# A remade head and a spread decay in a kernel that joins linear attention with a gelu layer

## The chip, the cores and the metric

The kernel runs on one core of one Trainium2 chip. Its time is the device time of one execution in microseconds, and the median of several executions is compared. A profile of one execution shows each instruction on the five engines and the transfers. The engines are TensorE (PE, with PEld for its weight loads), VectorE (DVE), ScalarE (ACT), GpSimd (POOL) and SyncE (SP).

## The reference

```python
# q, k, v: (4, 8, 768, 64); lam: (8,); block = 64
for b in range(nb):
    intra = einsum('bhic,bhjc->bhij', qb, kb) * Dmask
    intra = einsum('bhij,bhjd->bhid', intra, vb)
    inter = einsum('bhid,bhde->bhie', qb * lam_pow, kv_state)
    out[:, :, sl] = intra + inter
    kv_state = lam_block * kv_state + einsum('bhsd,bhse->bhde', kb * rev_pow, vb)
# then, with x of (3072, 512), w_in (512, 2048) and w_out (2048, 512):
h = x @ w_in
return (0.5 * h * (1.0 + erf(h / sqrt(2)))) @ w_out
```

Linear attention with a decay for each head gives x. Two matrix products with a gelu between them follow. The state `kv_state` is the only thing that one block of the sequence hands to the next.

## The kernel before, in words

The sequence of 768 is cut into six groups of 128 positions. A group holds all four batches, so it has 512 tokens. Per group the kernel makes transposed copies of q and k, scores on TensorE, masked scores on DVE, outputs on TensorE, the scaled outputs `x_t` on DVE, then the first layer (`mm1`), the gelu on ACT, and the second layer (`mm2`). State products (k against scaled v, `vs`) give the next group's states; from group 1 on DVE adds them to the old states in `tmp`, and ACT multiplies them by the decay (`decay`, L306, four instructions, one for each pair of heads).

There is no scheduler at run time. Each engine works its own instructions in the order in which the program text emits them, and that order is written by hand in strings, one letter per action:

- `LOADS1` is the order on POOL in the head: `K Q V` load group 0 (the digit is the pair of batches), `k q v` group 1, `i` and `w` load parts of w_in and w_out, `m` makes a part of the mask `m_p` for the second half of the heads (L171), and `s` scales v (L199). Each load of q, k or v is two DMAs of 128 KB, and each of w_in or w_out is one of 256 KB. All go through the one software queue of POOL. The first k and q are issued ahead of the string.
- `HEAD` is the order of group 0: `K`, `Q` transposes (L316), `S` scores (L349), `O` outputs (L370) and `x_t`, `z` the first state products (L393), `m` and `n` blocks of eight first-layer matmuls (L725) for the first and second pair of batches, `M` masks of the first half, `d` decay tables, `g` a one-element gelu, and `.` an idle matmul (L711) whose result nobody reads. It stands where TensorE would otherwise wait.
- `PHASE1` runs group 0's second layer in 16 parts (`p`, four matmuls of 512 columns, L505) among group 1's attention (`k q s o`), sums of weights on DVE (`i`, `w`, `t`) and scalings of v on ACT (`h`).
- `PHASE2` runs group 1's first layer (`m`, `n`) among group 2's attention and the loads of group 3 (`K Q V`). `z` and `Z` are the state products of groups 1 and 2, `y` and `Y` the decays behind them, and `c` a transpose by DMA on SP's queue.
- `PA`, `PB`, `PC` are the periods of groups 2, 3 and 4, and 5. In each, `a` is a product of four matmuls (L526) of the group's own first layer and `m` one of four (L688) of the second layer of the group before, both in a form with seven products in place of eight. `v` is a visit of the next group's attention, `h` scales v, `x` makes sums on DVE. The digits of `L2S` and `LA` are lags, counted in slots, by which DVE's sums are put behind.

Within a period's unit, product 5 writes bank uV, which ACT copies to `Vs` (L556). Product 1 writes uY, which ACT copies into uV (L548, the seed). Product 6 writes uY again, and so waits for the seed.

Of the kernel before, what the change touches and what calls it, by code (L numbers as in the profile page):

```python
# [7 lines left out]
F32 = mybir.dt.float32  # L8
# [6 lines left out]
def kernel(  # L15
# [11 lines left out]
    B, H, S, D = q.shape  # L27
# [3 lines left out]
    HP = H // 2  # L31
# [16 lines left out]
    V, A, P, G, SY = nc.vector, nc.scalar, nc.tensor, nc.gpsimd, nc.sync  # L48

    def bank(tag, shape, dtype=F32, name=None):  # L50
        return ps.tile(shape, dtype, tag=tag, name=name or "p_" + tag, bufs=1)


    done = set()
# [22 lines left out]
    def flush():  # L77
        while later_list:
            x = min(later_list)
            later_list.remove(x)  # L80
            x[2]()


    raw = {}
    dram = dict(q=q, k=k, v=v)

    def load(g, pair, name):
        if pair == 0:
            raw[g, name] = raw_pool.tile([128, B, H, D], BF16, tag="r" + name, name="raw_" + name, bufs=1 if name == "q" else 2)
        t = raw[g, name].rearrange("p (n a) h d -> p n (a h d)", n=2)[:, pair].rearrange("p (h t d) -> p h t d", h=H, t=2)  # L90
        for b in range(2):
            G.dma_start(t[b * 64:(b + 1) * 64].rearrange("p h t d -> p h (t d)"),
                        dram[name][2 * pair + b, :, g * C:(g + 1) * C, :].rearrange("h (p t) d -> p h (t d)", t=2))
        raw[g, pair, name] = t
# [30 lines left out]
    idle = consts.tile([128, 256], BF16)  # L125
# [24 lines left out]
    for hi in range(2):  # L150
        p = slice(hi * D, (hi + 1) * D)
# [36 lines left out]
    def new_x(g):  # L188
        xs[g] = x_pool.tile([128, HP, B, C], BF16, tag="x", name="x_t")
# [111 lines left out]
                decay(g + 1, raw["tmp", g])  # L301
        later(lag, add)

    def decay(g, tmp):
        for hp in range(HP):
            A.activation(states[g][:, :, hp, :], tmp[:, :, hp, :], ACT.Copy, scale=lam_c[:, hp:hp + 1])  # L306
        done.add(("st", g))


    def p_transposes(g, pair, name, tag, engs):  # L310
# [100 lines left out]
    def new_g(g):  # L411
        gts[g] = g_pool.tile([128, NK2, T], BF16, tag="g", name="g_t")

    def new_gs(g):
        gs[g] = [None if i == 2 else g_pool.tile([128, NK2 // 2, T // 2], BF16, tag=f"gs{i}", name=f"gs{i}", bufs=2) for i in range(4)]
        gs[g][2] = gts[g][:, 0:NK2 // 2, T // 2:]
# [28 lines left out]
    def sums_x(g, i):  # L445

        x = xs[g]
        if i == 3:
            t_x[g] = [x_pool.tile([128, 2, T // 2], BF16, tag=f"tx{i}", name=f"tx{i}", bufs=2) for i in range(4)]
        t1, t2, t3, t4 = (t.rearrange("p k (s c) -> p k s c", s=2) for t in t_x[g])  # L450
        b11, b12, b21, b22 = x[:, 0:2, 0:2], x[:, 0:2, 2:4], x[:, 2:4, 0:2], x[:, 2:4, 2:4]
        need(("x", g, 2), ("x", g, 3))
        if i != 3:
            need(("x", g, 0), ("x", g, 1))
        if i == 3:
            V.tensor_sub(t3, b22, b12)
        elif i == 1:
            V.tensor_sub(t1, b12, b11)
        elif i == 2:
            need(("tx", g, 1))  # L460
            V.tensor_sub(t2, b22, t1)
        else:
            need(("tx", g, 2))
            V.tensor_sub(t4, b21, t2)
        done.add(("tx", g, i))
# [227 lines left out]
        return slots  # L693


    LOADS1 = "Q1 m1 i0 V0 K1 m0 V1 i4 i1 i5 s0 i2 i3 w0 s1 i7 i6 k0 q0 w1 w4 w2 w5 k1 q1 v0 v1 w6 w3 w7"
    HEAD = "b . . . . . . . . . . . . . . . . . . . . . . . . . . . . K M M . . . . . . . Q d . . . . . . . S . S Q . . . . . . . . . . . . . . . . . . . . . . . . O . . . . . . . . . K . . . . . S . . . . . . . S . . m g O z . m n n n n m m m n m m n n n m"

    def script(text, actions):
        for word in text.split():  # L700
            fn = actions[word]
            (fn.pop(0) if isinstance(fn, list) else fn)()

    tags = ["uY", "uV", "uZ"]
    idle_ps = {}

    def idle_bank(tag):
        idle_ps[0] = bank(tag, [128, 512], F32, "idle_ps")

    def keep_warm():  # L710
        P.matmul(idle_ps[0][:, 0:256], idle[:, :128], idle, start=True, stop=True)  # L711

    part_no = [0]

    def mm1_part(g, i, pair, lag=None):

        need(*[("x", g, 2 * pair + b) for b in range(2)])
        h = bank(tags[part_no[0] % 3], [128, 2, 256])
        part_no[0] += 1
        x = xs[g].rearrange("p k s c -> p k (s c)")  # L720
        w = slice(256 * pair, 256 * pair + 256)
        for j in range(2):
            kf = 2 * i + j
            for ki in range(NK1):
                P.matmul(h[:, j, :], w_in_t[:, ki, kf * 128:(kf + 1) * 128], x[:, ki, w],  # L725
                         start=(ki == 0 and j == 0), stop=True, skip_group_check=True)
        A.activation(gts[g][:, 2 * i:2 * i + 2, w], h, ACT.Gelu)
        done.add(("gp", g, i, pair))
        u = i % 4
        if lag and all(("gp", g, x, y) in done for x in (u, u + 4) for y in range(2)):  # L730
            done.update(("g", g, u, n) for n in "XYZW")
            for n, j in enumerate((1, 2, 4, 3)):
                later(int(lag[4 * u + n]), lambda j=j: sums_g(g, u, j))
        tick()

    new_x(0)
    new_g(0)
    for item in LOADS1.split():
        i = int(item[1:])
# [8 lines left out]
        else:  # L748
            load(int(item[0].islower()), i, item[0].lower())
    script(HEAD, {  # L750
        ".": keep_warm,
# [33 lines left out]
        "z": lambda: p_state_products(1, ("a0", "a1")),  # L785
        "y": lambda: decay(2, raw["tmp", 1]),
    }
    PHASE1 = "i i p w i k q i p p w p s k q p p p t s p p w t s h h o w p p p s p p o p p"
    script(PHASE1, attn_1)


# [11 lines left out]
    new_g(1)  # L803
    new_gs(1)
    new_x(2)
    L2S = "2792133901460230"
    PHASE2 = "q z m k y n s q m n h s k n K m s o m n t V n s t Q h m n c c o x c M Z m c x m n m x x n Y"

    def digits(text, i, n):
        return [int(c) for c in text[i * n:(i + 1) * n]]  # L810

    script(PHASE2, {
        "m": [lambda i=i: mm1_part(1, i, 0, L2S) for i in (0, 4, 1, 5, 2, 6, 3, 7)],
        "n": [lambda i=i: mm1_part(1, i, 1, L2S) for i in (0, 4, 1, 5, 2, 6, 3, 7)],
        "w": attn_1["w"],
# [11 lines left out]
        "y": attn_1["y"],  # L827
        "M": mask_n,
        "Z": lambda: p_state_products(2, ab),
        "Y": lambda: decay(3, raw["tmp", 2]),  # L830
        "x": [lambda i=i: sums_x(2, i) for i in (3, 1, 2, 4)],
    })
    flush()

    PA = "mQKamammahmaavamaahmhahhmhmhmamhmaavammcVaaccmavmammmmaavcaaamavmamamaxaxxmmamxm"
    PB = "hQaKahhhhvmhmhhmVamvmaamamamamammaammacvacamamamccmavamammamavamamxmaamaaxxmammx"
    PC = "KQahamhvhhhmhhmVhmamamammaaavmmamamaacamcvmaacmcammvamaaammaamvammaaxmmaamxmmxax"
    LA = "2201000002202032034341212002332000200000022"  # L840
    LB = "2010000142522221213032570306003201000104020"
    LC = "0000001010210242003020330213002101104202001"
    for g in range(2, NG):
        seqs, lag = {2: (PA, LA), 5: (PC, LC)}.get(g, (PB, LB))
        LZ, LW, LS, LM, LV = lag[0:4], lag[4:8], lag[8:24], lag[24:28], lag[28:43]
        new_g(g)
        m2 = mm2_slots(g - 1, dict(M=digits(LM, 0, 4)))
        new_gs(g)
        att = g + 1 < NG
        if att:  # L850
            new_x(g + 1)
        assert seqs.count("a") == seqs.count("m") == 28
        a = []
        for u in range(4):
            sl = dict(zip("5162734", unit_slots(g, u, dict(Z=int(LZ[u]), W=int(LW[u]), S=digits(LS, u, 4)))))
            a += [sl[c] for c in ("1562734" if u == 0 else "5162734")]
        cross = list(CROSS)
        visits = list(range(5))
        sums = [3, 1, 2, 4]
        heads = list(range(H))  # L860
        for c in seqs:
            if c == "a":
                a.pop(0)()
                tick()
            elif c == "m":
                m2.pop(0)()
                tick()
            elif c == "v":
                i = visits.pop(0)
                if att:  # L870
                    visit(g + 1, i, digits(LV, i, 3))
            elif c in "KQV":
                if g + 2 < NG:
                    load_group(g + 2, c.lower())
            elif c == "c":
                x = cross.pop(0)
                if g + 2 < NG:
                    crossbar(g + 2, *x)
            elif c == "h":
                h = heads.pop(0)  # L880
                if att:
                    scale_v_group(g + 1, h)
            elif c == "x":
                i = sums.pop(0)
                if att:
                    sums_x(g + 1, i)
        assert not (a or m2 or visits or sums or heads or cross)
        flush()
    for s in mm2_slots(NG - 1, dict(M=(0, 0, 0, 0))):
        s()  # L890
# [32 lines left out]
```

## Time and profile before

| What | Value |
| --- | --- |
| median of 3 runs | 209.7 us (209.05 to 211.25) |
| the profiled execution | 210.08 us |
| its span, first to last instruction | 208.3 us |
| granted clock of TensorE, mean | 0.998 |
| busy: PE, DVE, ACT, POOL | 96%, 68%, 58%, 29% |
| instructions in the profile | 6283 |

The profiled execution's time is 1.8 us longer than the span, for what lies ahead of the first and behind the last instruction. A row of a timeline gives start, length, engine, line, operation, tiles and the number of merged instructions, and in brackets the engine's idle time ahead of it with what ended it. A row of the chain gives start, length and what. "issue" there is time in which an engine waited for nothing that the profile shows. A DMA row gives issues, the size of each and the median time from issue to landing.

### The profile page before, as it was taken

To read this page: it belongs to the slowest core of one execution; us is meant where nothing else is said; L and a number is where in the kernel's file an instruction comes from. 1 tells how busy PE (TensorE), PEld (TensorE's weight loads), DVE (VectorE), ACT (ScalarE), POOL (GpSimd) and SP (SyncE) were. 2 spreads that over 40 slices of the span, in tenths; PEclk is the share of its full clock that TensorE was granted. 3 is DMA by queue.
4 is the path that set the end of the run, shared out by engine and by line. 5 is a ranking of instruction groups with operands and counts; after the bars stand their busy time and mean duration, and the time that the engine had idled before them with its cause. 6 is when DMAs were issued, how large, how long until landed. Compare 5 with 4: busy or idle time off the path is not lost.

```text
span 208.3 us, 6283 instructions
## 1 busy us (share of the span) xinstructions
PE 200.1 (96%) x2699; PEld 162.2 (78%) x2699; DVE 142.3 (68%) x288; ACT 120.9 (58%) x247; POOL 59.8 (29%) x72
## 2 busy tenths in 40 slices
PE   7989699999999998999999999999999999999993
PEld 5767588554578897888888888888888888888882
DVE  3548641859666997698988498886699654765232
ACT  6433266364379868882589653688554566655210
POOL 7999937777072301800054000000000000000000
PEclk9999999999999999999999999999999999999999
DMA  5999999999979985999739994530003030011214
GB/s 53 145 158 186 185 186 196 161 171 179 208 142 158 146 101 78 81 159 146 178 55 196 158 148 55 151 104 0 3 0 101 3 105 0 0 53 65 86 53 151
DMA packets 81291, 23.47 MB, mean 113 GB/s; under 512 B 69488, under 2 KB 80752, under 8 KB 81264
## 3 DMA queue, kind: packets, MB, share of 16 engines
q0 software_dynamic: 62416, 13.64, 74.4%
q1 hardware_dynamic: 18848, 9.44, 20.7%
q8 instruction: 21, 0.34, 0.7%
q14 instruction: 6, 0.05, 0.1%
HBM read 27.27 MB, written 6.29 MB: 161 GB/s over the span
## 4 chain that ended last, share of the span: by engine, by line
PE 87%; DMA 3%; POOL 3%; ACT 2%; issue 2%; DVE 1%; POOLq 0%; ACTq 0%
PE p_mY L688 14%; PE p_uY L526 14%; PE p_mR L688 13%; PE p_uV L526 7%; PE p_uV L725 5%; PE p_uY L725 5%; PE p_uZ L725 4%; PE p_uZ L526 3%; DMA raw_v<-in_v_dram 3%; PE t_ps L316 2%; PE p_a L271 2%; PE p_a L243 2%; PE p_uY L505 2%; PE p_mY L505 2%; PE p_uZ L505 2%
## 5 line engine op out<-in xcount | busy, mean ns | idle before, releaser
L688 PEld LDWEIGHTS <-g_t 128*128 128x128 bf16 x304 | 29.5, 98 | 4.1 <-issue 0.4
L526 PEld LDWEIGHTS <-s_in 128*128 128x128 bf16 x256 | 24.4, 97 | 5.5 <-issue 2.2
L725 PEld LDWEIGHTS <-w_in_t 128*128 128x128 bf16 x256 | 24.5, 98 | 3.3
L688 PEld LDWEIGHTS <-gs 128*128 128x128 bf16 x240 | 23.2, 98 | 2.9
L688 PE MATMUL p_mY<-w_out_t,g_t 128*128 128x256 bf16 x160 | 20.8, 273 | 0.2 <-ACT o_q L657 0.2
L526 PEld LDWEIGHTS <-w_in_t 128*128 128x128 bf16 x192 | 18.6, 98 | 2.6
L526 PE MATMUL p_uY<-tx,s_in 128*128 128x256 bf16 x128 | 19.2, 272 | 1.0 <-ACT p_uV L548 1.0
L538 ACT ACTIVATE g_t<-p_uV 128x512 bf16<-128x512 f32 x16 | 9.5, 594 | 17.9 <-PE p_uV L526 17.6
L576 DVE TENSOR_TENSOR p_uZ<-p_uY,Vs 128x512 f32<-128x512 f32 x16 | 11.2, 698 | 10.6 <-PE p_uY L526 10.6
L356 DVE TENSOR_TENSOR sc_m<-p_a,m_p 128x512 bf16<-128x512 f32 x20 | 12.9, 684 | 6.4 <-PE p_a L349 6.3
L261 DVE TENSOR_TENSOR sc_m<-p_a,m_p 128x512 bf16<-128x512 f32 x24 | 15.6, 682 | 1.1 <-PE p_a L246 1.1
L585 DVE TENSOR_TENSOR Vs<-p_uY,Vs 128x512 f32<-128x512 f32 x16 | 11.0, 690 | 6.9 <-PE p_uY L526 6.7
L538 ACT ACTIVATE g_t<-Vs 128x512 bf16<-128x512 f32 x16 | 10.0, 628 | 9.7 <-DVE Vs L585 9.7
L711 PE MATMUL idle_ps<-idle 128*128 128x256 bf16 x91 | 14.2, 312 | 1.1 <-DVE idle L126 1.1
L98 POOL DMA_DIRECT2D raw_q<-in_q_dram x3 | 5.1, 1698 | 31.1 <-DMA qT<-raw_q 31.1
L475 DVE TENSOR_TENSOR gs<-g_t 128x512 bf16<-128x512 bf16 x20 | 8.4, 420 | 8.0 <-ACT g_t L538 7.9
L711 PEld LDWEIGHTS <-idle 128*128 128x128 bf16 x91 | 9.5, 112 | 3.9 <-DVE idle L126 1.1
L725 PE MATMUL p_uV<-x_t,w_in_t 128*128 128x256 bf16 x88 | 11.4, 273 | 0.0
L725 PE MATMUL p_uY<-x_t,w_in_t 128*128 128x256 bf16 x88 | 11.4, 273 | 0.0
L688 PE MATMUL p_mR<-t_out,gs 128*128 128x256 bf16 x80 | 11.4, 273 | 0.0
L322 ACT COPY kT<-t_ps 128x512 bf16<-128x512 bf16 x7 | 4.0, 586 | 12.7 <-DVE kT L324 10.8
L688 PE MATMUL p_mR<-w_out_t,g_t 128*128 128x256 bf16 x80 | 11.2, 273 | 0.0
(135 smaller groups left out, 451.6 us busy)
## 6 DMA issues: line engine op xcount, KB each, us to landing
w_in_t<-in_moe_w_in_dram POOLq DMA_DIRECT2D x8, 256.0 KB, 6.5
w_out_t<-in_moe_w_out_dram POOLq DMA_DIRECT2D x8, 256.0 KB, 8.2
raw_k<-in_k_dram POOLq DMA_DIRECT2D x12, 128.0 KB, 7.2
raw_q<-in_q_dram POOLq DMA_DIRECT2D x12, 128.0 KB, 6.9
raw_v<-in_v_dram POOLq DMA_DIRECT2D x12, 128.0 KB, 5.5
raw_k<-in_k_dram POOLq DMA_DIRECT2D x3, 512.0 KB, 9.3
raw_v<-in_v_dram POOLq DMA_DIRECT2D x3, 512.0 KB, 11.8
raw_q<-in_q_dram POOLq DMA_DIRECT2D x3, 512.0 KB, 9.1
```

Source lines behind the costliest of these rows:

```text
L98: G.dma_start(raw[g, name].rearrange("p b h d -> p (b h) d"), dram[name][:, :, g * C:(g + 1) * C, :].rearrange("b h si d -> si (b h) d"))
L261: V.tensor_mul(sc_m[g, s_sc][:, :, r, :], sc[r], m_nh[:, r])
L356: V.tensor_mul(sc_m[g, pair][half][:, :, hi], sc[hi], m_ph[:, hi, 2 * half:2 * half + 2])
L475: eng.tensor_add(s1, gLH, gHH)
L505: P.matmul(mo[io], gts[g][:, kf, io * C:(io + 1) * C], w_out_t[:, kf, :], start=(part == 0 and j == 0), stop=(part == 3 and j == 3))
L526: P.matmul(dst[:, b, :], w(ko, f0 + b * 128), x_of(ko), start=(start and b == 0 and ko == 0), stop=True, skip_group_check=True)
L538: A.activation(dst, src, ACT.Gelu)
L576: V.tensor_add(st["Z"], st["Y"], st["Vs"])
L585: V.tensor_add(st["Vs"], st["Y"], st["Vs"])
L688: P.matmul(st[dst][:, io, :], a(kf, io), b(kf), start=(new and u == 0 and io == 0 and kf == 0), stop=True, skip_group_check=True)
L711: P.matmul(idle_ps[0][:, 0:256], idle[:, :128], idle, start=True, stop=True)
L725: P.matmul(h[:, j, :], w_in_t[:, ki, kf * 128:(kf + 1) * 128], x[:, ki, w], start=(ki == 0 and j == 0), stop=True, skip_group_check=True)
```

## The change

It changes the strings of the order, the form of the idle matmul, and where group 3's decays are emitted.

- An idle matmul has 512 columns (two times the same 256) in place of 256, and 40 stand where 91 stood: 13 in place of 28 ahead of the first transposes, 9 in place of 24 ahead of the first outputs.
- In `LOADS1` the mask part `m1` goes behind the first v and the second k, `i4` goes ahead of the second v, `i2` ahead of `i1` and of the scaling `s0`, and `w3` ahead of `w6`.
- In `HEAD` the first state products `z` stand behind two more first-layer blocks (`m`, `n`) that come after the second outputs. Three more idle matmuls stand ahead of those outputs, and the one behind `z` goes. The words of the change say four blocks; the strings show two.
- In `PHASE1` one `p` and one `w` change places with `i`, `k`, `q`, and scalings and second-layer parts move by one place.
- In `PHASE2` group 3's v is loaded first, then k, then q; the order of `s`, `o`, `h`, `c`, `x` is slightly other; the decay `Y` at its end goes. The lags `L2S` and `LA` have other digits.
- In `PA` the four decays of group 3's states are emitted one by one (`Y`). The first slots are `m a a m m m a` with the seeds behind the second `a`, where they were `m a m a m m a`. The load of q for group 4 comes behind that of k.

```diff
-    def decay(g, tmp):
-        for hp in range(HP):
+    def decay(g, tmp, pairs=range(HP)):
+        for hp in pairs:
             A.activation(states[g][:, :, hp, :], tmp[:, :, hp, :], ACT.Copy, scale=lam_c[:, hp:hp + 1])
-        done.add(("st", g))
+        if HP - 1 in pairs:
+            done.add(("st", g))
...
-    LOADS1 = "Q1 m1 i0 V0 K1 m0 V1 i4 i1 i5 s0 i2 i3 w0 s1 i7 i6 k0 q0 w1 w4 w2 w5 k1 q1 v0 v1 w6 w3 w7"
-    HEAD = "b . . . . . . . . . . . . . . . . . . . . . . . . . . . . K M M . . . . . . . Q d . . . . . . . S . S Q . . . . . . . . . . . . . . . . . . . . . . . . O . . . . . . . . . K . . . . . S . . . . . . . S . . m g O z . m n n n n m m m n m m n n n m"
+    LOADS1 = "Q1 i0 V0 K1 m1 i4 m0 V1 i2 i1 i5 s0 i3 w0 s1 i7 i6 k0 q0 w1 w4 w2 w5 k1 q1 v0 v1 w3 w6 w7"
+    HEAD = "b . . . . . . . . . . . . . K M M . . . . Q d . . . . S S Q . . . . . . . . . O . . . . K . . S . S m . . . g O m n z n n n m m m n m m n m n n"
...
-        idle_ps[0] = bank(tag, [128, 512], F32, "idle_ps")
+        idle_ps[0] = bank(tag, [128, 2, 256], F32, "idle_ps")
...
-        P.matmul(idle_ps[0][:, 0:256], idle[:, :128], idle, start=True, stop=True)
+        P.matmul(idle_ps[0], idle[:, :128], idle[:, None, :].to_broadcast((128, 2, 256)), start=True, stop=True)
...
-    PHASE1 = "i i p w i k q i p p w p s k q p p p t s p p w t s h h o w p p p s p p o p p"
+    PHASE1 = "i i i w k q i p p p w p s k q p p p t s p p w t h s h o w p p p p s p p o p"
...
-    L2S = "2792133901460230"
-    PHASE2 = "q z m k y n s q m n h s k n K m s o m n t V n s t Q h m n c c o x c M Z m c x m n m x x n Y"
+    L2S = "2393225902261242"
+    PHASE2 = "q z m k y n s q m n h s k n V m K s o n m n t s h m t Q c n c o x c M x Z m m c n m x x n"
...
-        "Y": lambda: decay(3, raw["tmp", 2]),
...
-    PA = "mQKamammahmaavamaahmhahhmhmhmamhmaavammcVaaccmavmammmmaavcaaamavmamamaxaxxmmamxm"
+    PA = "mKaammmahmQvhYaaamaahYmamYhhmmaYhhhmmaavamcamVmcaacvmmammmaavcaaamavmamamaxaxxmmaxmm"
...
-    LA = "2201000002202032034341212002332000200000022"
+    LA = "2201100002302032034341221002332000000000022"
...
+        decays_left = list(range(HP)) if g == 2 else []
...
+            elif c == "Y":
+                hp = decays_left.pop(0)
+                decay(3, raw["tmp", 2], [hp])
```

More of the change, by code (lines that the diff above doesn't have):

```diff
@@ L886 @@
                     sums_x(g + 1, i)
-        assert not (a or m2 or visits or sums or heads or cross)
+            elif c == "Y":
+                hp = decays_left.pop(0)
+                decay(3, raw["tmp", 2], [hp])
+        assert not (a or m2 or visits or sums or heads or cross or decays_left)
         flush()
```

## The prediction

> **What bounds the kernel now.** I read the page first, then PE's waits, then the chain of work that ended last in two stretches of the head.
>
> ```profile
> PE 200.1 (96%) x2699; PEld 162.2 (78%) x2699; DVE 142.3 (68%) x288; ACT 120.9 (58%) x247; POOL 59.8 (29%) x72
> DMA  5999999999979985999739994530003030011214
> GB/s 53 145 158 186 185 186 196 161 171 179 208 142 158 146 101 78 81 159 146 178 55 196 158 148 55 151 104 0 3 0 101 3 105 0 0 53 65 86 53 151
> q8 instruction: 21, 0.34, 0.7%
> ```
>
> TensorE is busy for 96% of the span, and part of that is idle matmuls. The transfers are busy from the first slices up to about slice 12, some 60 us, at some 180 GB/s. So two things can be gained: time of PE that does nothing for the result, as long as the transfers allow it, and PE's own waits. These are few:
>
> ```profile
> PE p_mY L393 <- issue: 1.8, 1, 1.8
> PE p_uY L526 <- ACT p_uV L548: 1.0, 2, 0.7
> PE p_mR L370 <- DMA raw_v<-in_v_dram: 0.8, 1, 0.8
> ```
>
> One is a pause of 1.8 in the first state products that nothing in the profile explains, one a wait for ACT's seed, one the wait for the first v. The chain shows where they stand:
>
> ```profile
> 8.31 6.56 DMA raw_v<-in_v_dram
> ...
> 16.64 0.57 PE t_ps L316 x16
> ...
> 17.86 0.35 PE p_a L349 x16
> ...
> 19.75 0.87 PE p_uY L725 x8
> 20.62 0.59 PE p_a L370 x31
> ...
> 21.72 1.78 issue
> ...
> 37.05 0.86 PE p_mY L505 x4
> ...
> 41.98 1.01 PE t_ps L316 x32
> 42.99 0.97 PE p_mY L505 x4
> ```
>
> The landing of the first v at 14.87 (8.31 + 6.56) releases the first outputs. Then come idle products, the transposes at 16.64, the second outputs at 20.62, the pause, fifteen first-layer blocks (0.87 each, and one stands ahead of the outputs), and from 37.05 the second layer. From there to 78 PE never waits, so whatever the head gives is carried on as long as inputs have landed.
>
> **The first v.** POOL's timeline has the mask part ahead of the load:
>
> ```profile
> 5.83 1.10 POOL L171 TENSOR_TENSOR m_p<-cmask_p,lam_mp 128x512 f32<-128x512 f32 x1
> 6.83 0.82 POOL L110 DMA_DIRECT2D w_in_t<-in_moe_w_in_dram  x1
> 7.63 1.39 POOL L92 DMA_DIRECT2D raw_v<-in_v_dram  x2
> 10.34 1.11 POOL L171 TENSOR_TENSOR m_p<-cmask_p,lam_mp 128x512 f32<-128x512 f32 x1
> 11.33 1.43 POOL L92 DMA_DIRECT2D raw_v<-in_v_dram  x2
> 19.07 1.93 POOL L199 TENSOR_TENSOR vs<-raw_v,lam_mp 128x1024 bf16<-128x1024 bf16 x1
> ```
>
> With `m1` behind the second k, i0 and the first v are issued 1.0 earlier (6.83 less 5.83), so v lands near 13.9. Its bounds are 13.0, if the queue's other tail also goes, and 14.9, if transfers rather than issues set it. The last mask part moves to about 12.3 (i4's 0.8 is now ahead of it), and the two masked scores of the second half, 0.65 each by DVE's rows below, end near 13.6. So DVE would not let PE start much ahead of 13.6, and I take 13.9. Nine idle products of 512 columns replace 24 of 256:
>
> ```profile
> 11.15 2.79 PE L711 MATMUL idle_ps<-idle 128*128 128x256 bf16 x24
> 38.87 1.04 PE L505 MATMUL p_uY<-w_out_t,g_t 128*128 128x512 bf16 x4
> 39.74 1.03 PE L505 MATMUL p_uV<-w_out_t,g_t 128*128 128x512 bf16 x4
> ```
>
> Four matmuls of 512 columns take 0.87 from start to start, 0.22 each, so nine are 2.0 for the 2.8 before. They start at about 11.15 as before and end by 13.1, under the v's landing. The form costs nothing by itself: 512 columns cost what two times 256 do. In all, 40 x 0.22 = 8.7 stands for 91 x 0.11 = 10.
>
> **From the outputs to the second layer.** Outputs 0.6, four idle products 0.87: the transposes start at 15.4 in place of 16.64. Between them and the second outputs PE is not the limit. DVE is:
>
> ```profile
> 18.25 1.29 DVE L356 TENSOR_TENSOR sc_m<-p_a,m_p 128x512 bf16<-128x512 f32 x2 [0.58 <-PE p_a L349]
> 19.47 0.69 DVE L356 TENSOR_TENSOR sc_m<-p_mY,m_p 128x512 bf16<-128x512 f32 x1
> 20.08 0.68 DVE L356 TENSOR_TENSOR sc_m<-p_mR,m_p 128x512 bf16<-128x512 f32 x1
> ```
>
> The last masked score ends at 20.76, 4.1 behind the transposes' start at 16.64; fewer idle products in between save nothing. So the second outputs end near 19.8 (15.4 + 4.1 + 0.3), where they ended at 21.2. The second v, issued at 12.3 behind i4, must land by 19.3; before it was issued at 11.33. Its rows in the DMA view:
>
> ```profile
> raw_v<-in_v_dram POOLq DMA_DIRECT2D x2, 128.0 KB, 5.2
> ```
>
> With 5.2 from the later issue (13.0) it lands at 18.2, and with i4's 256 KB ahead of it, 1.4 at 180 GB/s, at 19.6 at the latest; I take no wait, and 0.3 at most. Then two blocks of 0.87 run ahead of the state products, to 21.5. POOL's second scaling of v, which those read, ended at 21.0 and moves 0.3 back, as one load more is ahead of it: 21.3, covered by the two blocks. Without them it would cost 1.5. The products take 0.5 and thirteen blocks of 0.87 (11.3) remain: the second layer starts at 33.4 in place of 37.05, **3.6 earlier**, if the pause goes.
>
> **The pause.** In this stretch the DMA view shows one packet of the instruction queue:
>
> ```profile
> q8 instruction: 1, 0.02, 5.9%
> ```
>
> That is the window 21.0 to 22.0. The page has 21 such packets of 0.34 MB in all, 16 KB each, and PE has 5398 matmuls and weight loads, 257 for each packet. PE stops after 59 of the 64 products, whose weight loads went out in 0.64:
>
> ```profile
> 20.97 0.64 PEld L393 LDWEIGHTS <-raw_k 64*64 64x64 bf16 x59
> ```
>  I read the pause as PE out of code, with the next piece late behind saturated transfers. The Trainium skill, Runtime: NRT & Kernel Launch, section "Instruction fetch mechanics", says that code is refilled in 16 KiB blocks of 256 instructions, which the packets here agree with, and that a crossing is mostly hidden. The 1.78 disagrees for this place; by the rule the pause would be no matter of code and would stay with `z`, 1.8 later at 35.2.
>
> 102 instructions of idle products go ahead of `z`. So the same count of instructions (the 705th) is reached not in `z` but in the fourth block behind it, near 24.6, and the 256 ahead of it then run from the second outputs on, some 5.3 us. Before, counted back, they ran from the scores at 17.86 to the pause at 21.7, 3.8 us, and the next piece was there 5.6 after their start, at 23.5. I take a leftover of 0.3; bounds 0 and 1.8. The second layer starts at **33.7**.
>
> **What the transfers allow.** Group 1's second k and q are the next to be waited for. POOL issues them here:
>
> ```profile
> 32.86 1.38 POOL L92 DMA_DIRECT2D raw_q<-in_q_dram  x2
> raw_q<-in_q_dram POOLq DMA_DIRECT2D x2, 128.0 KB, 7.3
> ```
>
> The second issue is at 33.5 (half of 1.38 on) and lands 7.3 later, at 40.9. Its transposes are the second half of the row at 41.98, so they start at 42.5, with a slack of 1.6. The change puts the same loads ahead of it, so in a full queue it lands earlier only by bubbles that go. The one that I see is the 1.0 ahead of i0, some of which is lost again to later scalings on POOL. I take 0.7 (bounds 0 and 1.3): 40.2. PE wants it 5.4 behind the second layer's start (42.5 less 37.05), at 39.1, so it waits 1.1, and the gain of 3.4 shrinks to **2.2** (42.5 less 40.3). The leftover of the pause lies inside that wait up to 1.1. Behind it come v, w_out and group 2's loads in the same queue, with more slack; I count nothing for them. `PHASE1` and `PHASE2` emit the same work in an order slightly other; PE has no wait in these stretches now, and DVE and ACT leave room, so I cost them at 0, bounds -0.3 and 1.
>
> **The decays.** The chain at the end of group 1's first layer:
>
> ```profile
> 78.44 0.60 ACT g_t L727
> 79.03 1.59 ACT state L306 x4
> 80.62 0.48 ACT Vs L556
> 81.12 0.58 ACT p_uV L548
> ```
>
> And PE's timeline there:
>
> ```profile
> 79.98 1.04 PE L688 MATMUL p_mY<-w_out_t,g_t 128*128 128x256 bf16 x8
> 81.75 0.60 PE L526 MATMUL p_uY<-tx,s_in 128*128 128x256 bf16 x4 [0.72 <-ACT p_uV L548]
> ```
>
> Four decays of 0.4 stand in ACT's order ahead of the copies of the first unit, and PE waits. Its next matmuls would have begun at 80.85 (eight at 0.109 from 79.98) and began at 81.75: 0.9. Without the four, the copies start at once behind product 5 and take 1.1, and three slots of 0.44 cover them, 0.1 short at most. So **0.8** comes back (bounds 0.5 and 0.9). Now each decay holds ACT for 0.4 somewhere in the period of group 2, where ACT is busy for two thirds; the second visit, which reads the states, comes four slots behind the last decay.
>
> **Sum.** 210.08 - 2.2 - 0.8 = 207.1 for a profiled execution, whose time is 0.4 above the median; against the median, 209.7 - 3.0 = **206.7**. About 1% (2.1 us) is what a measurement of this kernel can tell from no change.
>
> **Rivals.**
>
> A. The forecast, 206.7, its own range 205.7 to 208.2. Chance 0.52.
>
> B. Group 1's q lands by 39.1 (the first v's 1.3 of slow transfer goes as well), and PE sets the pace: 3.4 + 0.8 = 4.2, 205.5. Against it: the queue never runs empty behind i0. Chance 0.12.
>
> C. The pause comes again behind `z`, in full. PE then wants q at 39.1 + 1.5 = 40.6 and the gain is 1.9 + 0.8 = 2.7; with 1 more from a longer one, 1.7: 207.0 to 208.0. For it: transfers are saturated at 24.6 as at 21. Chance 0.14.
>
> D. The remade orders of group 2's period take it back: with decays, scalings and copies mixed in ACT's order, PE stops ahead of product 6 or of a visit in each of the four units as it did once, 0.72 each. 3.0 - 4 x 0.72 leaves about 0: 209.6. For it: the chain above. Against: PE shows no other wait there, at these loads. Chance 0.13.
>
> E. Slower: TensorE's clock. The first 28 idle products took 204 ns each and later ones 116:
>
> ```profile
> 1.06 5.71 PE L711 MATMUL idle_ps<-idle 128*128 128x256 bf16 x28 [1.06 <-DVE idle L126]
> ```
>
> So PE starts slow, and the idle products keep it fast. With 40 for 91 it could fall back at the wait for v and stay slow until the blocks run unbroken, as it did for the first 5.7. The 7.6 us of work from 13.9 to 21.5 would take near twice as long, 6.5 more; the gain is gone from 4.2 of delay on (3.4 + 0.8), so 2.3 net loss: 212.0. Against it: the pause of 1.78 was followed by blocks of 0.87, full speed, and no wait that I foresee is longer than 1.1. Chance 0.09. The Trainium skill, TensorE: Matmul & The Clock Gate, Part 1, names an idle window of about 3.4 us for the fall to half; by that rule E does not happen, and no wait in this trace is long enough to try it.
>
> **The numbers.** Faster by over 1%: A but for its upper end (0.45), B, and most of C (0.10): 0.67. Within 1%: the rest of A and C and most of D: 0.21. Slower: E and the tail of D: 0.12. The range 205.0 to 209.2 holds A, B and C and leaves out E and most of D.
>
> **What would show it.** The first outputs start near 13.9 and the second layer near 33.7. The pause is gone from L393. PE waits about 1 us at the second transposes of group 1 for raw_q. The wait of L526 for the seed near 79 is gone, and idle matmuls take 0.22 each. The argument is wrong if the second layer starts later than 35, if q lands later than 41, or if PE gets new waits of over 0.5 in group 2's period.

## The result, and the profile after

The changed kernel takes 207.78 us in the median of six executions (207.37 to 208.12), the kernel before 209.77 (209.05 to 211.25). The ratio is 0.990, with a 95% interval of 0.986 to 0.993. Forecast were 206.7 and a range of 205.0 to 209.2. The profiled execution has a span of 205.5, 2.8 less than before.

PE's waits in the profile after:

```profile
PE p_uV L726 <- DVE x_t L379: 1.2, 1, 1.2
PE idle_ps L712 <- DVE idle L126: 1.1, 1, 1.1
PE p_mR L371 <- DMA raw_v<-in_v_dram: 0.4, 1, 0.4
PE t_ps L317 <- DMA raw_q<-in_q_dram: 0.4, 1, 0.4
PE p_uY L527 <- ACT p_uV L549: 0.3, 1, 0.3
```

The pause of 1.8 in the state products is gone, the wait for the seed fell from 1.0 to 0.3, and there is a new wait of 1.2: a first-layer block for `x_t`. It stands right behind the second outputs, as the chain shows (start, length, what):

```profile
7.24 6.32 DMA raw_v<-in_v_dram
...
14.24 0.97 PE idle_ps L712 x4
15.21 0.63 PE t_ps L317 x16
...
18.43 0.65 PE idle_ps L712 x3
19.08 0.72 PE p_a L371 x32
19.80 0.02 issue
19.82 1.35 DVE x_t L379 x2
21.17 0.04 issue
21.21 0.93 PE p_uV L726 x7
22.14 0.87 PE p_uZ L726 x8
...
23.65 0.98 PE p_uY L726 x8
```

The wait of 0.4 for `raw_q` is for group 0's q, at 8.2; group 1's q is not waited for. PE's timeline has a detail that the chain merges:

```profile
19.37 0.41 PE L371 MATMUL p_a<-sc_m,raw_v 64*64 64x128 bf16 x14
19.71 0.28 PE L726 MATMUL p_uV<-x_t,w_in_t 128*128 128x256 bf16 x1
21.21 0.93 PE L726 MATMUL p_uV<-x_t,w_in_t 128*128 128x256 bf16 x7 [1.22 <-DVE x_t L379]
```

The block's first matmul runs at 19.71 and its second waits till DVE has written `x_t` of the second pair. But the block belongs to the first pair.

Group 1's transposes, the row at 41.98 before, and the start of group 2's period:

```profile
35.11 1.01 PE t_ps L317 x32
...
40.03 1.01 PE t_ps L317 x32
```

```profile
77.08 0.60 PE L527 MATMUL p_uV<-tx,s_in 128*128 128x256 bf16 x4
77.51 1.47 PE L689 MATMUL p_mY<-w_out_t,g_t 128*128 128x256 bf16 x12
78.95 0.60 PE L527 MATMUL p_uY<-tx,s_in 128*128 128x256 bf16 x4
```

The gain is 1.95 at the second transposes (41.98 less 40.03), and 2.80 at product 6 (81.75 less 78.95), which is the gain of the span. So 2.0 comes from the head and 0.8 from the decays, and nothing is lost or won later. This is one execution of each kernel. The profiled one of the kernel before lies 0.3 above its median and that of the changed kernel 0.4 below, so the medians are only 2.0 apart.

### The profile page after: what moved, and what is told of

The parts are those of the page before. It is cut to its first block, busy times and chain, and to the rows that moved or that the text cites. A ratio compares the mean times of both kernels' runs of the same rounds, so it can differ in the third digit from the quotient of the medians.

```text
span 205.5 us, 6178 instructions
## 1 busy us (share of the span) xinstructions
PE 198.2 (96%) x2643; PEld 156.5 (76%) x2648; DVE 141.7 (69%) x288; ACT 120.8 (59%) x247; POOL 59.7 (29%) x72
## 4 chain that ended last, share of the span: by engine, by line
PE 89%; DMA 3%; POOL 3%; DVE 2%; issue 1%; ACT 1%; POOLq 0%; ACTq 0%
PE p_mY L689 15%; PE p_uY L527 14%; PE p_mR L689 13%; PE p_uV L527 7%; PE p_uY L726 5%; PE p_uV L726 5%; PE p_uZ L726 4%; PE p_uZ L527 3%; DMA raw_v<-in_v_dram 3%; PE t_ps L317 2%; PE p_a L271 2%; PE p_a L243 2%; PE p_uV L506 2%; PE p_uY L506 2%; PE p_a L246 2%; PE p_a L350 2%
## 5 line engine op out<-in xcount | busy, mean ns | idle before, releaser
L689 PEld LDWEIGHTS <-g_t 128*128 128x128 bf16 x304 | 29.5, 98 | 4.1 <-issue 0.4
L712 PE MATMUL idle_ps<-idle 128*128 128x512 bf16 x40 | 12.3, 448 | 1.1 <-DVE idle L126 1.1
L557 ACT COPY Vs<-p_uV 128x512 f32<-128x512 f32 x16 | 9.4, 588 | 4.0 <-PE p_uV L527 4.0
L689 PE MATMUL p_mR<-w_out_t,gs 128*128 128x256 bf16 x80 | 11.0, 273 | 0.0
```

The source lines that it names most:

```text
L557: A.copy(st["Vs"], st["V"])
L689: P.matmul(st[dst][:, io, :], a(kf, io), b(kf), start=(new and u == 0 and io == 0 and kf == 0), stop=True, skip_group_check=True)
L712: P.matmul(idle_ps[0], idle[:, :128], idle[:, None, :].to_broadcast((128, 2, 256)), start=True, stop=True)
```

## The experiments

Ratios are to the kernel before, executed in the same group of runs. There are three groups, and a ratio of one is only roughly a ratio of another. Where the changed kernel was not executed in a group, "under the changed kernel" goes by its 207.78 and 207.71 from elsewhere.

**Is the pause a matter of code, and does it come again?** The kernel before was profiled again, and once with 24 instructions more ahead of the products.

> The kernel before, profiled once more. If the pause in the first state products is PE out of code behind saturated transfers, it comes again after 59 of the 64 products, but its length may differ by some tenths from 1.8. If it is a chance event it is gone.

> The kernel before with 12 of the 24 idle products ahead of the first outputs cut into 24 of 128 columns: the same columns, 24 instructions more. Code theory: the pause comes 24 instructions earlier among the state products, after 47 of the 64, and lasts about the same, 1.8. Rival: it stays after 59, or goes.

```diff
-Q . . . (24 idle products of 256 columns) O
+Q . . . (12 of 256 columns, then 24 of 128) O
```

PE's weight loads, first of the kernel before again, then with 24 instructions more:

```profile
20.76 0.64 PEld L393 LDWEIGHTS <-raw_k 64*64 64x64 bf16 x59
23.59 0.13 PEld L393 LDWEIGHTS <-raw_k 64*64 64x64 bf16 x5 [2.19 <-issue]
```

```profile
21.18 0.54 PEld L393 LDWEIGHTS <-raw_k 64*64 64x64 bf16 x47
22.51 0.23 PEld L393 LDWEIGHTS <-raw_k 64*64 64x64 bf16 x17 [0.80 <-issue]
```

The pause comes at the same product again, and with 24 instructions more it comes 12 products earlier, to the one. It hangs on the count of instructions, not on what they do. Its length is no constant: 1.8, 2.1 and 0.7 by PE's waits, and the execution with 0.7 took 209.2. In narrow windows of the DMA view the instruction queue's packet starts at 21.0, 21.2, 20.1 and, in the run of the loads below, 21.4. The rows of two of these windows, 21.0 to 21.1 of the kernel before and 20.0 to 20.1 of the one with 24 instructions more:

```profile
q8 instruction: 1, 0.02, 59.2%
```

```profile
q8 instruction: 1, 0.02, 59.4%
```

The pauses end at 23.5, 23.6, 22.5 and 23.8, so 2.4 to 2.5 later in all four. In all four PE stops behind the same count, 705 matmuls and weight loads. In the ten profiles without the pause it comes to this count 2.5 to 5.5 behind the start of the packet. So all fourteen fit the reading that PE has run out of code and waits for this piece. The fetch itself was not varied, and why its packet starts no earlier is not shown. The Trainium skill, Runtime: NRT & Kernel Launch, section "Instruction fetch mechanics", calls a crossing mostly hidden; here, with transfers at some 190 GB/s around it, this one was not.

The second profile of the kernel before shows a further price. PE's stretches of 3.4 us around the pause (busy of the engines, then granted clock, DMA share, GB/s):

```profile
21.60:25.00 3.40, 1.41 (x17) 1.25 (x18) 1.87 (x4) 0.04 (x1) 3.40 (x6) 1.00 1.36 196
25.00:28.40 3.40, 3.40 (x19) 2.40 (x17) 3.33 (x11) 1.37 (x3) 2.30 (x4) 0.50 1.52 182
28.40:31.80 3.40, 3.40 (x33) 3.04 (x32) 0.29 (x1) 2.18 (x4) 2.58 (x5) 1.00 1.53 191
```

Behind the pause the granted clock is 0.50 for one stretch, PE does 19 matmuls in it where it later does 33, and some 1.7 us are lost (211.84 in this execution). In the runs of this study 13 of 58 executions of the kernel before (7 of 19, 4 of 13 and 2 of 26 in the three groups) had a mean clock of 0.989 to 0.992, and they took 210.4 to 212.5, where the others had medians of 209.1 to 209.4. Of 14 executions of the changed kernel none was below 0.997.

The pause alone does not decide it. In the run of the loads below the pause is the longest, 2.3, and PE is busy for less of the same stretch, 1.19, but the clock holds:

```profile
21.60:25.00 3.40, 1.19 (x15) 1.05 (x16) 1.42 (x3) 0.00 (x0) 3.40 (x6) 1.00 1.33 191
25.00:28.40 3.40, 3.40 (x34) 3.05 (x32) 3.33 (x10) 2.39 (x4) 2.35 (x4) 1.00 1.58 178
```

None of that kernel's ten executions was below 0.999. One of ten of the changed kernel with the old loads, whose profile has no pause, was at 0.989. Only one execution with the lower clock was profiled, so that the pause brings the others about is not shown.

**Fewer instructions alone.**

> The kernel before with all its idle products of 512 columns and half as many; nothing else. Code theory: 88 instructions fewer stand ahead of the state products, so the end of the piece of code falls some five blocks behind them, and the pause in L393 is gone. In its place PE waits about 0.9 for x_t (DVE, done near 22.6) at the block behind the products, so the time falls by 0.9, ratio 0.996. Rival, that the pause belongs to the products themselves: it stays, 1.5 to 2 us, ratio 1.000.

```diff
-        P.matmul(idle_ps[0][:, 0:256], idle[:, :128], idle, start=True, stop=True)
+        P.matmul(idle_ps[0], idle[:, :128], idle[:, None, :].to_broadcast((128, 2, 256)), start=True, stop=True)
```

208.83 against 209.76; the ratio is 0.997 (0.993 to 1.001). Against the twelve executions of the kernel before with a full clock (median 209.35) it is 0.5. Its waits:

```profile
PE p_mY L393 <- POOL vs L199: 0.5, 1, 0.5
PE p_a L393 <- issue: 0.2, 1, 0.2
```

The pause is gone, as the code theory has it. The wait that takes its place is for POOL's scaling, 0.5, and none is for `x_t`. The interval just reaches 1, so the time alone shows no gain; but the pause is gone by nothing but the form and count of matmuls that compute nothing.

**The other parts alone.**

> The kernel before with the changed order of loads alone. Theory: the first outputs start near 13.6 in place of 14.9, all behind them in the head comes about 1.1 earlier, the pause stays, group 1's second q lands near 39.5; time -1.1, ratio 0.995. Rival, that the transfers set the end of the head whatever their order: q lands at 40.9 as before and the time changes by less than 0.3.

209.43 against 209.76, ratio 1.001 (0.997 to 1.005): nothing. PE waits 2.3 in the pause, which ends at 23.8:

```profile
PE p_mY L393 <- issue: 2.3, 1, 2.3
PE t_ps L316 <- DMA raw_k<-in_k_dram: 0.3, 1, 0.3
```

The first v did land earlier in this profile, at 14.05, but the next transposes, held up by k, came only 0.4 earlier, and the longer pause took that back. The number of the rival came true, but not its reason: the first layer ended at 37.4 by the pause, and q landed at 40.1, ahead of PE.

> The kernel before with the first state products behind two more blocks, and nothing else (the one idle product behind them goes, since its bank is a block's by then). Theory: the end of the piece of code falls 32 instructions earlier among the products, after 43 of the 64, and is reached later, so the pause shrinks to some 0.3; but the block ahead of them waits 1.2 for x_t, which the products and the pause covered before. Together 0.0 to -0.4 where the clock holds, and fewer executions with a lower clock, so -0.6 in the median. Rival, that the place of the products is what the change gains by: -1.5.

```diff
-m g O z . m n n n n
+m g O m n z n n n
```

209.24 against 209.23, ratio 1.000 (0.997 to 1.002). Moving the products alone gains nothing, neither the rival's 1.5 nor the 0.6 expected of the median. The pause is gone and the wait for `x_t` has its place:

```profile
PE p_uV L725 <- DVE x_t L378: 1.2, 1, 1.2
```

**Parts undone in the changed kernel.**

> The changed kernel with group 3's four decays together at the end of group 1's first layer, as before, and not spread. Theory: they hold ACT for 1.6 ahead of the copies of the first unit, PE waits 0.8 to 0.9 ahead of product 6, time +0.8 against the changed kernel. Rival, that the order with three second-layer products behind the second first-layer product covers them: no wait, +0.1.

```diff
-PHASE2 = "... m x x n"      PA = "mKaaammm...Y...Y..."
+PHASE2 = "... m x x n Y"    PA without its four Y
```

208.69, ratio 0.994 (0.990 to 0.998), where the changed kernel has 0.990 and 0.992; 0.9 slower than its medians. The wait is back at product 6, which comes 39.7 behind the second transposes (80.53 less 40.82), where it was 38.9 in the changed kernel (78.95 less 40.03), so 0.8 later as expected:

```profile
80.53 0.60 PE L527 MATMUL p_uY<-tx,s_in 128*128 128x256 bf16 x4 [0.73 <-ACT p_uV L549]
```

> The changed kernel with the first state products directly behind the second outputs, as before, and the two blocks behind them. By the prediction's step (the two blocks cover POOL's second scaling of v) it is 1.2 slower. By the trace of after (the block behind the outputs waits 1.2 for x_t whatever it is, and POOL's scaling ends at 21.0) the products use that wait, and the kernel is 0.4 faster than the changed one: wait for POOL 1.0, none for x_t.

```diff
-S m . . . g O m n z n n n
+S m . . . g O z m n n n n
```

206.89 in four executions, ratio 0.984 (0.976 to 0.991). Their spans are all 205.1, and those of fourteen executions of the changed kernel 205.1 to 206.5. PE waits 0.9 for POOL's scaling and not at all for `x_t`:

```profile
PE p_mY L394 <- POOL vs L199: 0.9, 1, 0.9
```

The first layer ends 0.4 earlier than in the profile after (34.72 for 35.11), and the span is 0.4 less. So the move of the state products, taken by itself, is a loss in the changed kernel.

> The changed kernel with the order of loads of before. If the new order lands the first v 1.0 earlier, this is 1.0 slower than the changed kernel. By the runs so far (v lands at 13.1 to 14.4 with the new order, at 13.4 to 15.1 with the old one; the new order alone changed nothing) transfers set the landing, and this is within 0.4 of it.

208.58, ratio 0.997 (0.994 to 0.999), and in the same group the changed kernel once more:

> The changed kernel once more, to compare the other runs of this group with it on one chip: 207.8 by all theories, ratio 0.990 to the kernel before, no run with TensorE's clock below 0.995, and the wait of 1.2 for x_t at the block behind the second outputs.

207.71, ratio 0.992 (0.989 to 0.995). Old loads are 0.9 slower, so here the order of loads is worth about what was forecast for it, and the expectation of less than 0.4 failed. In this profile v lands at 14.7 (8.31 + 6.38), 1.1 and 1.4 later than in the two profiles of the changed kernel:

```profile
8.31 6.38 DMA raw_v<-in_v_dram
```

One profile is a weak witness here: v lands at 13.4 to 15.1 in the six profiles with the old order (mean 14.4) and at 13.1 to 15.2 in the eight with the new one (mean 13.9). That the loads alone gained nothing because the pause stood behind them fits both results, but is argued, not shown.

**What is the wait for `x_t`?**

> The changed kernel with x_t of group 0 laid out pair by pair, so that what the first pair's block reads lies in no way between what the second pair's scaling writes. Theory: the first layer's block behind the second outputs reads only the first pair, and its wait of 1.2 for x_t is one for memory that it does not read, by where the two lie; it goes, the blocks come 1.2 earlier, q (39.4) is then waited for 0.3, time -0.9 against the changed kernel. Rival, that the wait is for something else that ends then: it stays, 0.0.

```diff
-dst = xs[g][:, w, 2 * pair + b, :]
+dst = x_pairs(g)[:, pair, w, b, :]      # group 0: pair, k, s, c in memory
```

207.45, ratio 0.986 (0.978 to 0.994). PE's timeline:

```profile
20.26 1.05 PE L729 MATMUL p_uV<-x_t,w_in_t 128*128 128x256 bf16 x8
21.79 1.05 PE L729 MATMUL p_uZ<-x_t,w_in_t 128*128 128x256 bf16 x8 [0.48 <-DVE x_t L382]
```

The first pair's block no longer waits, so its wait was one for memory that it does not read: the write of the second pair strides over the whole tile, and the reads of the second to fourth part lie between its pieces. I had forgotten that the next block is one of the second pair and waits by right, here 0.5; so the expected 0.9 was too much. The wait is what this run shows; a gain in time it does not show, as 0.3 of median is within the spread. In its profile the second v landed at 19.65, and the second outputs began 0.6 later than in the profile after.

> The changed kernel with the second first-layer block ahead of the second outputs, in place of three idle products, and the state products right behind the outputs. Theory: in that place the block waits for no x_t; outputs 0.2 later, products wait for POOL till 21.0, the next block starts at 21.4; the first layer ends 1.3 earlier, q is waited for 0.3, time -1.0 against the changed kernel. Rival, that transfers set the pace: 0.0.

```diff
-S m . . . g O m n z n n n
+S m m g O z n n n n
```

206.65 in four executions (206.44 to 209.25), ratio 0.985 (0.975 to 0.995), about 1.1 under the changed kernel, with three of the four at 206.4 to 206.8. The profiled one was the longest, and its waits say why:

```profile
PE t_ps L317 <- DMA raw_q<-in_q_dram: 1.5, 1, 1.5
PE p_mY L394 <- POOL vs L199: 1.2, 1, 1.2
PE p_uV L726 <- DMA w_in_t<-in_moe_w_in_dram: 1.0, 1, 1.0
```

With PE earlier, transfers are next: weights and group 1's second q land late in this execution (29.5 and 42.0).

**All of it together.**

> The changed kernel with x_t of group 0 laid out pair by pair, two blocks of the first pair ahead of the second outputs and of the state products, one more behind the outputs (of weights that have landed), the blocks of the last weights at the end, and one second-layer part between group 1's second k and q. Theory: no wait for x_t and almost none for POOL, the second layer starts 2.2 earlier; then q's landing (38.6 to 41) takes back up to 0.7: 206.1, ratio 0.982, 1.7 under the changed kernel. Rival, that transfers set the pace of the whole head: 0.5 under the changed kernel.

```diff
-S m . . . g O m n z n n n m m m n m m n m n n
+S m m g O m z n n n n m m n m n m n m n
```

206.30 in six executions (206.02 to 207.57), ratio 0.986 (0.983 to 0.989), 1.4 under the changed kernel in the same group, nearer to the 1.7 expected than to the rival's 0.5. That it is faster than the two kernels above is not shown: their ratios are 0.984 and 0.985. The profiled execution was again the longest; there group 0's second q landed late, at 12.5, and PE waited 2.6 of these 3.2 for it:

```profile
PE t_ps L320 <- DMA raw_q<-in_q_dram: 3.2, 2, 2.6
```

## Why the prediction was right, step by step

The sum, 3.0, stands against 2.8 in the span and 2.0 in the first medians, so the medians gained a third less than forecast. Both terms that were left at the end were right in size in this pair of profiles, 2.2 (measured 1.95) and 0.8 (0.8). But the first came about in another way, by two errors that cancelled, and that is luck. By its own signs the argument of the head was wrong: the second layer started at 36.1, later than 35 (the first layer ended at 35.11, and group 1's first transposes now come between), and PE did not wait for group 1's q.

- **The first v.** Forecast to land near 13.9, it landed at 13.56. The reason given, that the issue sets it, holds only in part. The weights i0 were issued 1.0 earlier and landed no earlier (5.80 + 6.3 = 12.1, where it was 6.83 + 5.1 = 11.9), so transfers and not the issue set their landing. The DMA views of these issues, before and then after:

```profile
w_in_t<-in_moe_w_in_dram POOLq DMA_DIRECT2D x1, 256.0 KB, 5.1
```

```profile
w_in_t<-in_moe_w_in_dram POOLq DMA_DIRECT2D x1, 256.0 KB, 6.3
```

- **The pause.** Its cause and its going were forecast, with a leftover of 0.3; measured 0. Fifty idle matmuls fewer stand ahead of the products, so 100 instructions and not 102. The 705th was put near 24.6 and comes at 26.65, behind a packet that starts at 21.98. It needs no move of the products: the wide idle products alone do it, and so does the move alone.
- **The two blocks.** This step failed. It had them as cover for POOL's scaling, free of waits. The first of them waited 1.2, and the products ended at 23.65 in place of 22.0. The row that would have told it was missing because the pause and the products covered that wait before. The price of the pause was counted as pure loss, 1.8, though `x_t` lay under it.
- **The transfers.** This step failed the other way. It took 1.1 off the gain (it counted from 40.3, though q was put at 40.2), and nothing was taken off: 1.94 at the end of the first layer (37.05 less 35.11), 1.95 at the second transposes. q was forecast for 40.2, and landed by 39.4:

```profile
30.97 1.35 POOL L92 DMA_DIRECT2D raw_q<-in_q_dram  x2
raw_q<-in_q_dram POOLq DMA_DIRECT2D x2, 128.0 KB, 7.7
```

PE came to its transposes 1.4 later than forecast (40.5, half way in the row at 40.03, in place of 39.1) and found it landed. Had PE come at 39.1, it would have waited 0.3. The bound is near in one execution: the kernel with a block ahead of the outputs waits 1.5 for this q, which landed at 42.0 there. The reworked head found it landed, and its waits for q are for group 0's.

- **The decays.** The chain was read rightly: the copies of the first unit start at once, three slots cover them, and each single decay costs nothing. Rival D did not happen.
- **The clock.** Rival E, a fall of the clock in the changed kernel, did not happen. It happens in the kernel before, in 13 of 58 executions. That its pause "was followed by blocks of 0.87, full speed" was true of one execution. In the median of before there is thus a share of such losses, which the sum has no term for. The comparison gives 2.0 in the first group and 1.5 in another, there 1.4 (209.11 less 207.71) without the two executions at the lower clock.

## What to carry to other kernels

A pause that the profile puts down to nothing can hang on the count of instructions: shift the count by a known number and see whether it moves by as many. Ask what lies under a stall before counting its length as gain, since the next thing may be late there by nearly as much. When a wait appears for a tile that a matmul should not need, look at how the writer's pieces lie in memory around what is read.

## What was not expected of the hardware

A pause of PE of 2.1 us, in a stretch of 3.4 where it was busy for 1.4, was followed by a granted clock of 0.50 for about 3.4 us. The Trainium skill, TensorE: Matmul & The Clock Gate, Part 1, has the fall to half behind an idle window of about 3.4 us and the return behind a busy one as long. The length of the stretch at half clock agrees; the idle time ahead of it was shorter here. The pause of 1.8 in another execution (1.62 busy in the same stretch) and the one of 2.3 in the run of the loads (1.19 busy) had no such effect, and what made the difference stays open.

The landing of the first v moved from profile to profile with no change to what is issued ahead of it. In the kernel with a block ahead of the outputs and in the reworked head, issued alike at 7.25, it took 5.9 and 8.0, so it landed at 13.1 and 15.2:

```profile
raw_v<-in_v_dram POOLq DMA_DIRECT2D x2, 128.0 KB, 5.9
```

```profile
raw_v<-in_v_dram POOLq DMA_DIRECT2D x2, 128.0 KB, 8.0
```
